# Mixture of experts behind windowed attention: weights in pairs of blocks, a fifth round turned by VectorE

## The chip, the cores and the metric

The kernel runs on one core of a Trainium2 chip. The metric is device time in microseconds (us), the median over the runs shown. A profile is one more execution, recorded by the hardware profiler: TensorE (PE), VectorE (DVE), ScalarE (ACT), GpSimd (POOL), SyncE (SP, which here only issues DMAs) and the DMA queues.

## The reference

Attention over 8 batches of 8 heads (576 positions, 64 columns a head), four heads with a window of 32 positions and four with 32 positions at a stride of 4. Its output, 4608 rows of 512 columns, is the input of a layer with 8 experts, in which each row goes to one expert and each expert takes exactly 576 rows:

```python
    logits = x @ w_gate
    flat = logits.flatten()
    order = np.argsort(-flat)
    for idx in order:
        tok, e = (int(idx) // E, int(idx) % E)
        if assigned[tok] >= 0 or counts[e] >= cap:
            continue
        assigned[tok] = e
        counts[e] += 1
    for e in range(E):
        mask = assigned == e
        h = np.maximum(x[mask] @ w1[e], 0.0)
        out[mask] = h @ w2[e]
```

An expert's w1 is 512 x 1024 and its w2 1024 x 512, both float32, 2 MB each.

## The kernel before, in words

**Attention** (`attention`) fills the first 175 us, writes its rows x to DRAM (`xd`) and keeps the gate's logits. Nothing in it is changed.

**Rounds.** In each of eight rounds the router finds the expert that fills next and the list of its 576 rows. A round's search is eight steps, one after the other: nine small matmuls on PE (`counts`, L835) and a DVE chain of about 2 us (`step`, from L880). Then the expert's number goes to SP's registers (`fetch`), and the list is built (`settle`, `listing`: DVE compares, 18 small matmuls at L1174 into `ptx`, then `idx` at L1200). Later rounds' searches run while earlier experts are computed.

**Rows.** POOL gathers the listed rows in five blocks (four of 128 rows, one of 64) by indirect DMAs. For the matmuls they must stand with the 512 columns on the partitions. In the first five rounds (`gather`) PE transposes them: four matmuls a block at L1391 into PSUM. From round QUARTERS = 5 on (counted from 0: the sixth) `spread` does it without PE: gathered rows go to a buffer (two alternate), from there to a DRAM scratch (L1415), come back in four quarters of the columns (L1419), and DVE turns them in blocks of 32 x 32 (L1425). The columns then stand in another order on the partitions, so w1 is read from a second copy in that order, `w1q`. In both ways ACT rounds the block to `xh` and DVE computes the rest, `xl` (L1237, L1238). There is one `xh` and one `xl`, so these splits wait until the expert before has read its rows for the last time.

**Weights** (`weights`). A block is 128 x 512 values, 256 KB; w1 and w2 have eight blocks each. SP loads it into a `raw` buffer (L1255; eight for w1, four for w2), ACT rounds it to the high part, DVE subtracts to get the low part. In the first expert's w2 and the second's w1 and w2 (`ADDED`) DVE is spared: ACT writes the negated high part (L1264) and a DMA issued by POOL adds `raw` to it (L1266). Each part has eight buffers, one expert's worth. In the first two rounds a POOL memset of one element of a `raw` buffer (L1246), queued behind the gathers, holds the loads from block 3 or 4 on (`AHEAD_W`), since the load of that buffer, and all that SP has queued behind it, waits for it.

**Products** (`expert`). First product: for each of eight blocks f of the hidden layer and two column ranges j (256 and 320 rows of x), twelve matmuls into `ph` (L1455): high by high, low by high, high by low, over four parts of the 512 columns. ACT takes relu and rounds (`hb`), DVE the rest (L1476). Second product: for each of the five blocks of rows, over the eight f, three matmuls (L1500; two for the block of 64 rows, L1503 and L1505) into `py`, from where ACT copies and POOL scatters to the output.

**The order** is made when the kernel is built: each operation is listed with its engine, a cost, what it depends on and a boost; `Schedule.run` gives every engine its next operation by due time, and lets one that would be due later go first where it fits into idle time (up to a tolerance, 100 ns on DVE). The engines then execute their queues in order and wait by semaphores for the data alone. Costs given there decide the order and nothing else. B_W is the boost of weights, B_C that of a search, lower from round QUARTERS on.

Of the kernel before, what the change touches and what calls it, by code (L numbers as in the profile page):

```python
# [8 lines left out]
F32 = mybir.dt.float32  # L9
F32R = mybir.dt.float32r  # L10
# [4 lines left out]
AF = mybir.ActivationFunctionType  # L15
OP = mybir.AluOpType
# [6 lines left out]
DM = H * D  # L23
NE, FF = 8, 1024
# [14 lines left out]
TOL_DVE, TOL_ACT, TOL_POOL, TOL_PE, T_W = 100, -50, 200, 500, 730  # L39
T_P, T_S, AHEAD = 310, 2200, 5  # L40
B_L, B_G, B_T, B_X, B_H, B_HL, B_Y, B_S, B_W = 23000, 27000, 15000, 0, 20000, 17000, 28000, -15000, 1500
RAW1, D_R, NQ, AHEAD_W = 8, 262, (2, 2), (3, 4)
KB, QUARTERS, POOLED, T_B, T_H, B_R = 8, 5, range(0), 5000, 2500, 20000
ADDED, T_A, T_G, T_L = (("2", 0), ("1", 1), ("2", 1)), 4500, 4500, 3500
NS, B_E, DIRECT = (2, 2), 3000, 7
B_C = (0, 2500, *(20000 + -16000 * (r >= QUARTERS) for r in range(2, 8)))
# [1158 lines left out]
def moe(tc, ctx, C, R, xd, ROWS, w1, w1q, w2, out):  # L1205
    nc = tc.nc
# [4 lines left out]
    NF, ND = FF // 128, DM // 128  # L1211
# [6 lines left out]
    def ring(pool, shape, dtype, name, n):  # L1218
        return Ring([pool.tile(shape, dtype, name=f"{name}{i}") for i in range(n)])
# [1 line left out]
    PHR = [ring(ps, [128, 512], F32, f"ph{j}", 2) for j in range(2)]  # L1221
    PYR = ring(ps, [128, DM], F32, "py", 2)
    PTR = ring(ps, [128, 512], F32, "ptx", 1)
    RAW = {n: ring(pw, [128, 512], F32, "raw" + n, k) for n, k in (("1", RAW1), ("2", 4))}
    WH, WL = ({n: ring(pw, [128, 512], F32R, "w" + n + x, NF) for n in ("1", "2")} for x in "hl")
    XG = [pw.tile([128, DM // (1 + (i == 4))], F32, name=f"xg{i}") for i in range(NM + 2)]
    XU = [[] for _ in XG]
    XH, XL = (pw.tile([128, ND, CAP], F32R, name=n) for n in ("xh", "xl"))
# [9 lines left out]
    sub = lambda e, o, a, b: e.tensor_tensor(o, a, b, op=OP.subtract)  # L1238
    E, gemm1_end, x_users, got, gate = {}, {}, {}, {}, {}

    def weights(n, r, f, deps):

        raw, old, use = RAW[n].take()
        if n == "1" and r < len(AHEAD_W) and f == AHEAD_W[r]:

            gate[r] = op("POOL", 100, lambda: nc.gpsimd.memset(raw[:1, :1], 0.0), [got[r, 1], *old], B_G)  # L1246
        if r in gate:
            deps = [*deps, gate[r]]

        def load():  # L1250
            if n == "1":
                src = (w1 if r < QUARTERS else w1q)[bass.ds(E[r], 1), f].rearrange("o p d f -> p (o d f)")
            else:
                src = w2[bass.ds(E[r], 1), f * 128:f * 128 + 128, :].rearrange("o p d -> p (o d)")
            nc.sync.dma_start(raw, src)  # L1255

        ld = op("SP", 60, load, [*deps, *old], dma=T_W, lat=T_L if n == "1" and r == 1 and r in gate else 0)
        h, oldh, useh = WH[n].take()
        l, oldl, usel = WL[n].take()
        first = n == "1" and r == 0  # L1260
        hi = op("ACT", 525, lambda: act(h, raw), [ld, *oldh, st["rows"] if first else None], B_W)
        if (n, r) in ADDED:
            use.append(hi)
            ne = op("ACT", 525, lambda: nc.scalar.activation(l, h.bitcast(F32), AF.Copy, scale=-1.0), [hi, *oldl], B_W)  # L1264
            useh.append(ne)
            lo = op("POOL", 1040, lambda: nc.gpsimd.dma_start(l, raw, accum_op=OP.add), [ne], B_W, lat=T_A)  # L1266
            use.append(lo)
        elif n == "2" and r >= 2 and f in POOLED:
            lo = op("POOL", 1350, lambda: sub(nc.gpsimd, l, raw, h), [ld, hi, *oldl], B_W)
            use += [hi, lo]  # L1270
        else:
            lo = op("DVE", 600, lambda: sub(nc.vector, l, raw, h), [ld, hi, *oldl, st["list"] if first else None], B_W)
            use += [hi, lo]
        useh.append(lo)
        return h, l, hi, lo, useh, usel


    def chain(eng, cost, fn, deps, boost=None):
        return op(eng, cost, fn, deps, B_C[len(scan)] if boost is None else boost)
# [262 lines left out]
    def round_(r):  # L1542
        e = None
        if r:
            e = search(r) if r < NE - 1 else chain("DVE", 980, R.last, [st["fetch"], st["need"]])
        en = st["fetch"] = EN[r] = op("SP", 100, lambda: fetch(r, R.eidx), [e])
        ix, BOX[r] = settle(r, e)
        X[r] = gather(r, ix, BOX[r])
        if r < NE - 2:
            lv, gf = st["next"]  # L1550
            oc = (chain("ACT", 1055, lambda: R.copies(R.oh, nc.scalar), [lv]) if r else
                  chain("DVE", 640, lambda: R.copies(R.oh, nc.vector), [lv]))
            st["next"] = [oc, gf]
        W[r] = [weights("1", r, f, [en]) for f in range(NF)]

    round_(0)
    for r in range(NE):
        W2 = [weights("2", r, f, [EN[r], X[r][-1][0] if r == 1 else None]) for f in range(NF)]
        expert(r, X[r], BOX[r], W[r], W2)
        if r + 1 < NE:  # L1560
            round_(r + 1)
# [8 lines left out]
def layout(inputs):  # L1570
# [3 lines left out]
    seq = lambda x: x[:, 4:].reshape(B, 4, SR, DIL, D).transpose(0, 1, 3, 2, 4).reshape(B, 4, S, D)  # L1574
    rowwise = lambda x: ones(x.transpose(0, 2, 1, 3)).reshape(B, NB, 64, 4 * (D + 1)).transpose(0, 2, 1, 3).reshape(B, 64, -1)
    ones = lambda x: np.concatenate([x, np.ones(x.shape[:-1] + (1,), x.dtype)], -1)
    cb, _, cf, _ = consts()
    d = {
        "in_qp": plain(q[:, :4]), "in_kp": plain(k[:, :4]), "in_vp": rowwise(v[:, :4]),
        "in_qd": plain(seq(q)), "in_kd": plain(seq(k)), "in_vd": rowwise(seq(v)),  # L1580
        "in_moe_w_gate": np.asarray(inputs["moe_w_gate"]),
        "in_moe_w1": w1.reshape(NE, DM // 128, 128, FF // 128, 128).transpose(0, 3, 2, 1, 4),
        "in_moe_w1q": w1.reshape(NE, 4, DM // 128, 32, FF // 128, 128).transpose(0, 4, 1, 3, 2, 5).reshape(NE, FF // 128, 128, DM // 128, 128),
        "in_moe_w2": w2,
        "in_cb": cb, "in_cf": cf,
    }
# [54 lines left out]
```

## Time and profile before

| what | us |
| --- | --- |
| median of three runs | 658.03 |
| the runs | 656.75, 658.03, 662.26 |
| the profiled execution | 661.16 |
| its span, first to last instruction | 659.4 |

The profiled execution is one run with the profiler on; its durations belong to its own 661.16 us. A row that groups instructions gives line, engine, operation, tile written and tiles read, the count, then busy time, mean duration, and idle time before them. Matmuls overlap in PE's pipeline, so a matmul's duration is longer than the distance from its start to the next one's.

### The profile page before, as it was taken

What the parts mean: (1) busy time and instruction counts of PE and PEld (TensorE: products, weight loads), DVE (VectorE), ACT (ScalarE), POOL (GpSimd) and SP (SyncE); (2) the same over time, 40 slices, a digit from 0 to 9 for tenths busy, and PEclk for the clock granted to TensorE, in tenths of its full rate; (3) what the DMA queues carried; (4) which work ended last, traced back from release to release, by engine and by line L of the source; (5) the groups of instructions that cost most, each with busy time, mean ns of one, the idle gap of its engine ahead of it and who ended that gap; (6) DMA issues with size and microseconds to landing.
All of it is one profiled execution on the core that took longest, in us unless ns stands there. A gap on an engine that the chain in (4) does not pass through costs nothing.

```text
span 659.4 us, 18449 instructions
## 1 busy us (share of the span) xinstructions
PE 622.0 (94%) x7140; PEld 543.8 (82%) x7142; DVE 463.4 (70%) x1560; ACT 307.1 (47%) x675; POOL 208.4 (32%) x316
## 2 busy tenths in 40 slices
PE   6899899999748999999999999999999999999996
PEld 4788788888545988898799789879978988988985
DVE  4677577876676784689799888989898864724210
ACT  5667567566203824765336245325415624524311
POOL 6447555745003316434103113012212133011011
PEclk8999899999957999999999999999999999999999
DMA  8988699885106737997127135217714977403001
GB/s 237 261 234 239 205 280 260 257 214 178 45 33 215 150 68 205 250 193 267 67 71 247 61 93 194 85 52 252 216 57 161 281 243 229 127 32 105 1 25 48
DMA packets 61448, 106.11 MB, mean 161 GB/s; under 512 B 8368, under 2 KB 25264, under 8 KB 61360
## 3 DMA queue, kind: packets, MB, share of 16 engines
q1 hardware_dynamic: 52016, 79.75, 40.2%
q0 software_dynamic: 9344, 25.17, 14.3%
q8 instruction: 56, 0.92, 0.6%
q14 instruction: 32, 0.26, 0.2%
HBM read 76.19 MB, written 22.41 MB: 150 GB/s over the span
## 4 chain that ended last, share of the span: by engine, by line
PE 84%; DVE 5%; issue 5%; DMA 2%; ACT 2%; POOL 1%; SPq 0%; POOLq 0%; DVEq 0%; ACTq 0%
PE ph L1455 32%; PE py L1500 24%; PE px L543 5%; PE pS L531 4%; PE px L602 3%; PE py L1503 2%; PE py L1505 2%; PE pz L835 2%; PE ptx L1391 1%; PE pS L526 1%; PE pm L519 1%; PE pm L515 1%; PE pz L919 1%; PE px L628 1%; PE pm L468 1%
## 5 line engine op out<-in xcount | busy, mean ns | idle before, releaser
L1500 PE MATMUL py<-w2h,hb 128*128 128x512 f32 x512 | 168.6, 397 | 0.0
L1455 PE MATMUL ph<-xh,w1h 128*128 128x256 f32 (+1 forms) x512 | 138.7, 302 | 0.0
L1455 PE MATMUL ph<-xh,w1l 128*128 128x256 f32 (+1 forms) x512 | 136.8, 298 | 0.0
L1455 PE MATMUL ph<-xl,w1h 128*128 128x256 f32 (+1 forms) x512 | 136.4, 297 | 0.0
L1500 PEld LDWEIGHTS py<-w2h,hb 128*128 128x128 f32 x512 | 96.1, 188 | 19.0
L1237 ACT ACTIVATE hb<-ph 128x256 fp32r<-128x256 f32 (+2 forms) x192 | 59.8, 346 | 86.9 <-PE ph L1455 85.9
L1500 PE MATMUL py<-w2l,hb 128*128 128x512 f32 x256 | 99.8, 390 | 0.0
L1526 POOL DMA_INDIRECT out<-y,idx x40 | 39.7, 994 | 186.0 <-ACT y L1237 141.3
L1455 PEld LDWEIGHTS ph<-xh,w1h 128*128 128x128 f32 x512 | 92.0, 191 | 0.5
L1455 PEld LDWEIGHTS ph<-xh,w1l 128*128 128x128 f32 x512 | 92.1, 191 | 0.0
L1455 PEld LDWEIGHTS ph<-xl,w1h 128*128 128x128 f32 x512 | 92.1, 191 | 0.0
L1476 DVE SCALAR_TENSOR_TENSOR hb<-ph,hb 128x320 fp32r<-128x320 f32 (+1 forms) x128 | 57.0, 454 | 30.5 <-ACT hb L1237 29.4
L1237 ACT ACTIVATE y<-py 128x512 f32<-128x512 f32 (+1 forms) x40 | 23.9, 597 | 108.5 <-PE py L1500 95.1
L485 ACT ACTIVATE E<-pS 128x384 f32<-128x384 f32 x96 | 44.7, 491 | 28.0 <-PE pS L531 27.3
L1500 PEld LDWEIGHTS py<-w2l,hb 128*128 128x128 f32 x256 | 48.2, 188 | 8.6
L543 PE MATMUL px<-v,E 128*64 128x65 f32 x1152 | 48.7, 224 | 5.2 <-issue 3.8
L531 PE MATMUL pS<-q,k 128*64 128x64 f32 x1152 | 52.6, 227 | 0.5 <-issue 0.5
L543 PEld LDWEIGHTS px<-v,E 128*64 128x64 f32 x1152 | 42.4, 137 | 9.8 <-issue 5.8
L311 POOL COPY v<-v 32x520 f32<-32x520 f32 (+2 forms) x56 | 34.2, 633 | 46.6 <-DMA v<-in_vp 17.1
L531 PEld LDWEIGHTS pS<-q,k 128*64 128x64 f32 x1152 | 48.0, 142 | 0.7 <-issue 0.7
L1238 DVE TENSOR_TENSOR w2l<-raw,w2h 128x512 fp32r<-128x512 f32 x48 | 31.8, 685 | 18.8 <-ACT w2h L1237 17.8
L1237 ACT ACTIVATE w1h<-raw 128x512 fp32r<-128x512 f32 x64 | 38.6, 627 | 3.4 <-DMA raw<-in_moe_w 3.4
(218 smaller groups left out, 1121.4 us busy)
## 6 DMA issues: line engine op xcount, KB each, us to landing
raw<-in_moe_w SPq DMA_DIRECT2D x104, 256.0 KB, 4.4
raw<-in_moe_w1q SPq DMA_DIRECT2D x24, 256.0 KB, 4.3
qs<-in_qp SPq DMA_DIRECT2D x16, 288.0 KB, 3.8
k<-in_kp SPq DMA_DIRECT2D x16, 288.0 KB, 4.5
qs<-in_qd SPq DMA_DIRECT2D x16, 288.0 KB, 5.7
k<-in_kd SPq DMA_DIRECT2D x16, 288.0 KB, 5.1
xd<-xs SPq DMA_DIRECT2D x8, 512.0 KB, 5.7
w2l<-raw POOLq DMA_DIRECT2D x16, 256.0 KB, 4.3
```

The lines of the kernel that those rows point to most:

```text
L311: f(t[:32, c0 + 1:c1 + 1], t[96:, c0:c1])
L485: e = self.op("ACT", 475, lambda j=j, pS=pS: nc.scalar.activation(self.E[:, 3 * j:3 * j + 3].rearrange("p c x -> p (c x)"), pS.tile[:, :38 ...
L531: x = nc.tensor.matmul(pS[64 * h:64 * h + 64, k, :, h], self.K[:, 32 * g:32 * g + 64], self.Q[:, g], start=False, stop=True, skip_group_ch ...
L543: x = nc.tensor.matmul(px[64 * h:64 * h + 64, c - c0, a], self.E[:, k, 64 * a:64 * a + 64], self.V[:, k, 2 * self.ui + a], start=True, sto ...
L602: x = nc.tensor.transpose(pt.tile[:, 128 * (c - c0):128 * (c - c0) + 128], xs[:, c, 2 * ui:2 * ui + 2].rearrange("p a d -> p (a d)"), C["i ...
L835: nc.tensor.matmul(o, self.ohr[:, j].rearrange("p r x -> p (r x)"), self.G[:, 4 * j:4 * j + 4, :w], start=(j == 0), stop=(j == NCH // 4 - 1))
L1237: act = lambda o, i, f=AF.Copy: nc.scalar.activation(o, i, f)
L1238: sub = lambda e, o, a, b: e.tensor_tensor(o, a, b, op=OP.subtract)
L1455: nc.tensor.matmul(o, a[:, d * 128:d * 128 + 128], b[:, d, c0:c1], start=((d, i) == pairs[0]), stop=((d, i) == pairs[-1]))
L1476: hl = op("DVE", 335 if j == 0 else 400, lambda: nc.vector.scalar_tensor_tensor(hb[:, CAP + c0:CAP + c1], o, 0.0, hb[:, c0:c1], op0=OP.max ...
L1500: nc.tensor.matmul(py, x, w, start=(f + i == 0), stop=(f == NF - 1 and i == 2))
L1526: s = nc.gpsimd.indirect_dma_start(out=out, out_offset=bass.IndirectOffsetOnAxis(ap=box[0][:n, m:m + 1], axis=0), in_=y[:n], in_offset=None)
```

## The change

A weight tile becomes 128 x 1024, two blocks: one DMA of 512 KB, one ACT operation for the high part, one DVE operation (or ACT and adding DMA) for the low part, and products use halves of it. `raw` buffers keep their bytes (four for w1, two for w2), as do the parts (four tiles each). w1 lies in DRAM in pairs, so that a partition's 1024 values are contiguous; w2 is read as two rows of 512. `AHEAD_W` becomes (2, 2): the memset holds the third pair. QUARTERS becomes 4: the fifth round's rows go through the DRAM scratch and are turned by DVE, that expert reads `w1q`, and that round's search gets the lower boost. The costs given to the scheduler change with the sizes. A way to split on POOL that no tile used is gone.

```diff
-RAW1, D_R, NQ, AHEAD_W = 8, 262, (2, 2), (3, 4)
-KB, QUARTERS, POOLED, T_B, T_H, B_R = 8, 5, range(0), 5000, 2500, 20000
+RAW1, D_R, NQ, AHEAD_W = 8, 262, (2, 2), (2, 2)
+KB, QUARTERS, T_B, T_H, B_R = 8, 4, 5000, 2500, 20000
...
-    RAW = {n: ring(pw, [128, 512], F32, "raw" + n, k) for n, k in (("1", RAW1), ("2", 4))}
-    WH, WL = ({n: ring(pw, [128, 512], F32R, "w" + n + x, NF) for n in ("1", "2")} for x in "hl")
+    RAW = {n: ring(pw, [128, 1024], F32, "raw" + n, k) for n, k in (("1", RAW1 // 2), ("2", 2))}
+    WH, WL = ({n: ring(pw, [128, 1024], F32R, "w" + n + x, NF // 2) for n in ("1", "2")} for x in "hl")
...
-    def weights(n, r, f, deps):
+    def weights(n, r, g, deps):
 
         raw, old, use = RAW[n].take()
-        if n == "1" and r < len(AHEAD_W) and f == AHEAD_W[r]:
+        if n == "1" and r < len(AHEAD_W) and g == AHEAD_W[r]:
...
-                src = (w1 if r < QUARTERS else w1q)[bass.ds(E[r], 1), f].rearrange("o p d f -> p (o d f)")
+                src = (w1 if r < QUARTERS else w1q)[bass.ds(E[r], 1), g].rearrange("o p x -> p (o x)")
+                nc.sync.dma_start(raw, src)
             else:
-                src = w2[bass.ds(E[r], 1), f * 128:f * 128 + 128, :].rearrange("o p d -> p (o d)")
-            nc.sync.dma_start(raw, src)
-
-        ld = op("SP", 60, load, [*deps, *old], dma=T_W, lat=T_L if n == "1" and r == 1 and r in gate else 0)
+                src = w2[bass.ds(E[r], 1), g * 256:g * 256 + 256, :].rearrange("o (u p) d -> p (o u) d", p=128)
+                nc.sync.dma_start(raw.rearrange("p (u d) -> p u d", u=2), src)
+
+        ld = op("SP", 60, load, [*deps, *old], dma=2 * T_W, lat=T_L if n == "1" and r == 1 and r in gate else 0)
...
-        hi = op("ACT", 525, lambda: act(h, raw), [ld, *oldh, st["rows"] if first else None], B_W)
+        hi = op("ACT", 950, lambda: act(h, raw), [ld, *oldh, st["rows"] if first else None], B_W)
...
-            lo = op("DVE", 600, lambda: sub(nc.vector, l, raw, h), [ld, hi, *oldl, st["list"] if first else None], B_W)
+            lo = op("DVE", 1140, lambda: sub(nc.vector, l, raw, h), [ld, hi, *oldl, st["list"] if first else None], B_W)
...
-        return h, l, hi, lo, useh, usel
-
+        return [(h[:, x:x + 512], l[:, x:x + 512], hi, lo, useh, usel) for x in (0, 512)]
...
-        W[r] = [weights("1", r, f, [en]) for f in range(NF)]
+        W[r] = [x for g in range(NF // 2) for x in weights("1", r, g, [en])]
```

Three places show how the order moves. In the names below, `raw10` to `raw17` are w1's raw buffers and `raw20` to `raw23` w2's.

SP's queue at the first expert, before: the three first blocks of w1, then the load that waits for POOL's memset, and everything else behind it.

```order
L1255 DMA raw11_3702<-in_moe_w1 128x512
L1255 DMA raw12_3703<-in_moe_w1 128x512
L1255 DMA raw13_3704<-in_moe_w1 128x512 [waits Pool_49]
L1255 DMA raw14_3705<-in_moe_w1 128x512
L1255 DMA raw20_3709<-in_moe_w2 128x512
L1255 DMA raw21_3710<-in_moe_w2 128x512
```

The same place now; the row ahead of these loads `raw10`.

```order
L1253 DMA raw11_3702<-in_moe_w1 128x1024
L1256 DMA raw20_3705<-in_moe_w2 128x2x512
L1256 DMA raw21_3706<-in_moe_w2 128x2x512
L1253 DMA raw12_3703<-in_moe_w1 128x1024 [waits Pool_49]
L1253 DMA raw13_3704<-in_moe_w1 128x1024
```

Two pairs of w2 have moved ahead of the load that waits.

PE's queue in the fourth expert's second product, before (`w2h`, `w2l` are the parts of w2, `hb` the hidden layer, `xg` gathered rows):

```order
L1500 MATMUL py_3699<-w2h_3726,hb_3756 128x512
L1500 MATMUL py_3699<-w2l_3742,hb_3756 128x512
L1391 MATMUL ptx_3700<-const_63,xg_3745 128x128 x4
L1500 MATMUL py_3699<-w2h_3727,hb_3757 128x512
L1500 MATMUL py_3699<-w2l_3743,hb_3757 128x512
```

The same products now:

```order
L1497 MATMUL py_3699<-w2h_3713,hb_3734 128x512
L1497 MATMUL py_3699<-w2l_3721,hb_3734 128x512
L1497 MATMUL py_3699<-w2h_3714,hb_3735 128x512
L1497 MATMUL py_3699<-w2l_3722,hb_3735 128x512
```

The transposition is gone, and so are the four others of that round; the searches between these products stay.

DVE's queue at the end of the third expert's first product, before, from the list of the fourth round (`idx`) on; rows of the search and the list are left out. `hb4` and `hb5` are the last two hidden blocks.

```order
L1476 SCALAR_TENSOR_TENSOR hb4_3758<-ph00_3694,hb4_3758 128x256
L1238 TENSOR_TENSOR w2l3_3740<-raw23_3712,w2h3_3724 128x512
L1200 SCALAR_TENSOR_TENSOR idx_6291<-t1_6292 64x5 x2
L1238 TENSOR_TENSOR w2l4_3741<-raw20_3709,w2h4_3725 128x512
L1238 TENSOR_TENSOR w2l5_3742<-raw21_3710,w2h5_3726 128x512
L1238 TENSOR_TENSOR w2l6_3743<-raw22_3711,w2h6_3727 128x512
L1238 TENSOR_TENSOR w2l7_3744<-raw23_3712,w2h7_3728 128x512
```

The same place now:

```order
L1473 SCALAR_TENSOR_TENSOR hb4_3736<-ph00_3694,hb4_3736 128x256
L1200 SCALAR_TENSOR_TENSOR idx_6195<-t1_6196 64x5 x2
L1238 TENSOR_TENSOR w2l0_3719<-raw20_3705,w2h0_3711 128x1024
L1238 TENSOR_TENSOR w2l1_3720<-raw21_3706,w2h1_3712 128x1024
L1473 SCALAR_TENSOR_TENSOR hb5_3737<-ph01_3695,hb5_3737 128x256
L880 STREAM_TRANSPOSE Q_6249<-pz_92 128x128
L1238 TENSOR_TENSOR w2l2_3721<-raw20_3705,w2h2_3713 128x1024
L1238 TENSOR_TENSOR w2l3_3722<-raw21_3706,w2h3_3714 128x1024
```

Before, the splits of blocks 0 to 2 had gone long ago; now the first pair of the eight blocks stands behind the list, and the third pair, which uses the first one's raw buffer, behind a step of the next search.

## Rows read from the trace of the kernel before

**Rows 1.** The page: the span, and section 1, busy us and share.

```profile
span 659.4 us, 18449 instructions
...
PE 622.0 (94%) x7140; PEld 543.8 (82%) x7142; DVE 463.4 (70%) x1560; ACT 307.1 (47%) x675; POOL 208.4 (32%) x316
```

**Rows 2.** Windows by stage: stretch, length, busy us per engine, PE's clock, DMA share, GB/s.

```profile
208.70:268.00 59.30, 59.28 (x420) 52.63 (x416) 40.81 (x151) 30.92 (x65) 20.94 (x27) 0.97 0.68 170
...
386.50:444.20 57.70, 57.70 (x424) 50.43 (x421) 50.57 (x184) 23.39 (x52) 11.33 (x15) 1.00 0.35 115
...
552.00:603.10 51.10, 51.10 (x306) 46.22 (x305) 24.16 (x44) 21.15 (x50) 7.41 (x14) 1.00 0.36 109
```

**Rows 3.** Windows: the first 3.5 us of products (same columns).

```profile
208.77:212.28 3.51, 3.51 (x22) 3.39 (x18) 3.13 (x11) 1.12 (x2) 0.00 (x0) 0.51 0.98 312
```

**Rows 4.** PE's waits, 190 to 660 us: us in total, times, longest.

```profile
PE ptx L1180 <- POOL rx L1160: 3.5, 1, 3.5
PE ptx L1391 <- DMA xg<-xd,idx: 2.0, 1, 2.0
PE py L994 <- DVE pra L992: 0.8, 1, 0.8
```

**Rows 5.** Timeline of PE at a transposition: start, us, instruction.

```profile
417.94 0.60 PE L1391 MATMUL ptx<-const,xg 128*128 128x128 f32 x4
418.29 0.48 PE L1500 MATMUL py<-w2h,hb 128*128 128x512 f32 x1
418.61 0.39 PE L1500 MATMUL py<-w2l,hb 128*128 128x512 f32 x1
418.84 0.62 PE L1500 MATMUL py<-w2h,hb 128*128 128x512 f32 x2
```

**Rows 6.** Groups of instructions by form: busy us, mean ns, idle before.

```profile
L1237 ACT ACTIVATE w1h<-raw 128x512 fp32r<-128x512 f32 x64 | 38.6, 627 | 3.4 <-DMA raw<-in_moe_w 3.4
...
L1238 DVE TENSOR_TENSOR w1l<-raw,w1h 128x512 fp32r<-128x512 f32 x56 | 37.0, 687 | 0.1
...
L1425 DVE STREAM_TRANSPOSE xg<-xg 128x512 f32<-128x512 f32 x12 | 8.3, 701 | 0.7 <-DMA xg<-rows 0.7
...
L972 ACT ACTIVATE ohr<-oh 128x1152 bf16<-128x1152 bf16 x5 | 5.8, 1161 | 1.9 <-DVE oh L951 1.9
...
L1093 DVE TENSOR_TENSOR Lt<-Lt,cap 128x288 f32<-128x288 f32 x6 | 2.8, 459 | 0.2
```

**Rows 7.** Windows of 1 us at the start of the experts (columns as in rows 2).

```profile
196.00:197.00 1.00, 0.26 (x6) 0.36 (x7) 1.00 (x2) 0.78 (x2) 0.81 (x2) 0.50 0.75 238
197.00:198.00 1.00, 1.00 (x21) 0.99 (x20) 0.87 (x2) 0.20 (x1) 0.52 (x1) 0.50 0.96 342
...
202.00:203.00 1.00, 1.00 (x5) 0.29 (x3) 0.93 (x5) 0.00 (x0) 0.69 (x2) 0.98 0.66 209
```

**Rows 8.** Timeline of POOL, 199 to 207 us: the first of five gathers, and the memset.

```profile
199.72 1.45 POOL L1377 DMA_INDIRECT xg<-xd,idx  x1 [2.20 <-DVE idx L1192]
...
206.62 0.09 POOL L1246 MEMSET raw<- 1x1 f32 x1
```

**Rows 9.** Timeline of PE, 203 to 209.5 us: third transposition, first products.

```profile
208.03 0.63 PE L1391 MATMUL ptx<-const,xg 128*128 128x128 f32 x4 [1.99 <-DMA xg<-xd,idx]
...
208.77 1.12 PE L1455 MATMUL ph<-xh,w1h 128*128 128x256 f32 x4
```

**Rows 10.** Tile w2l on DVE, 320 to 362 us: ns min/median/max, first and last start.

```profile
L1238 DVE TENSOR_TENSOR w2l<-raw,w2h x8: 677/681/684, 327.2 to 358.3; 128x512 fp32r<-128x512 f32 x8
```

**Rows 11.** Timeline of DVE: the end of the fourth round's list.

```profile
352.46 0.33 DVE L1200 SCALAR_TENSOR_TENSOR idx<-t 64x5 int32<-64x5 f32 x2
```

**Rows 12.** Tile raw on SP, 297 to 300 us, then 206 to 212 us.

```profile
DMA to landing us min/median/max: 2.6/3.3/4.3
...
DMA to landing us min/median/max: 3.3/4.6/5.0
```

**Rows 13.** Timeline of PE: the third expert's second product begins.

```profile
355.39 0.39 PE L1500 MATMUL py<-w2h,hb 128*128 128x512 f32 x1
```

**Rows 14.** Tile w2l on POOL, 274 to 294 us: the adding DMAs.

```profile
DMA to landing us min/median/max: 3.3/4.5/5.1
```

More of the change, by code (lines that the diff above doesn't have):

```diff
@@ L1260, in weights @@
         first = n == "1" and r == 0
-        hi = op("ACT", 525, lambda: act(h, raw), [ld, *oldh, st["rows"] if first else None], B_W)
+        hi = op("ACT", 950, lambda: act(h, raw), [ld, *oldh, st["rows"] if first else None], B_W)
         if (n, r) in ADDED:
             use.append(hi)
-            ne = op("ACT", 525, lambda: nc.scalar.activation(l, h.bitcast(F32), AF.Copy, scale=-1.0), [hi, *oldl], B_W)
+            ne = op("ACT", 950, lambda: nc.scalar.activation(l, h.bitcast(F32), AF.Copy, scale=-1.0), [hi, *oldl], B_W)
             useh.append(ne)
-            lo = op("POOL", 1040, lambda: nc.gpsimd.dma_start(l, raw, accum_op=OP.add), [ne], B_W, lat=T_A)
+            lo = op("POOL", 1040, lambda: nc.gpsimd.dma_start(l, raw, accum_op=OP.add), [ne], B_W, lat=T_A + T_W)
             use.append(lo)
-        elif n == "2" and r >= 2 and f in POOLED:
-            lo = op("POOL", 1350, lambda: sub(nc.gpsimd, l, raw, h), [ld, hi, *oldl], B_W)
-            use += [hi, lo]
         else:
-            lo = op("DVE", 600, lambda: sub(nc.vector, l, raw, h), [ld, hi, *oldl, st["list"] if first else None], B_W)
+            lo = op("DVE", 1140, lambda: sub(nc.vector, l, raw, h), [ld, hi, *oldl, st["list"] if first else None], B_W)
             use += [hi, lo]
         useh.append(lo)
-        return h, l, hi, lo, useh, usel
+        return [(h[:, x:x + 512], l[:, x:x + 512], hi, lo, useh, usel) for x in (0, 512)]
     def chain(eng, cost, fn, deps, boost=None):
@@ L1553, in round_ @@
             st["next"] = [oc, gf]
-        W[r] = [weights("1", r, f, [en]) for f in range(NF)]
+        W[r] = [x for g in range(NF // 2) for x in weights("1", r, g, [en])]
     round_(0)
     for r in range(NE):
-        W2 = [weights("2", r, f, [EN[r], X[r][-1][0] if r == 1 else None]) for f in range(NF)]
+        W2 = [x for g in range(NF // 2) for x in weights("2", r, g, [EN[r], X[r][-1][0] if r == 1 else None])]
         expert(r, X[r], BOX[r], W[r], W2)
@@ L1576, in layout @@
     ones = lambda x: np.concatenate([x, np.ones(x.shape[:-1] + (1,), x.dtype)], -1)
+    pairs = lambda x: x.reshape(NE, FF // 256, 2, 128, DM).transpose(0, 1, 3, 2, 4).reshape(NE, FF // 256, 128, 2 * DM)
     cb, _, cf, _ = consts()
@@ L1581, in layout @@
         "in_moe_w_gate": np.asarray(inputs["moe_w_gate"]),
-        "in_moe_w1": w1.reshape(NE, DM // 128, 128, FF // 128, 128).transpose(0, 3, 2, 1, 4),
-        "in_moe_w1q": w1.reshape(NE, 4, DM // 128, 32, FF // 128, 128).transpose(0, 4, 1, 3, 2, 5).reshape(NE, FF // 128, 128, DM // 128, 128),
+        "in_moe_w1": pairs(w1.reshape(NE, DM // 128, 128, FF // 128, 128).transpose(0, 3, 2, 1, 4)),
+        "in_moe_w1q": pairs(w1.reshape(NE, 4, DM // 128, 32, FF // 128, 128).transpose(0, 4, 1, 3, 2, 5)),
         "in_moe_w2": w2,
```

## The prediction

> **What bounds the kernel now.** I read the page's busy times first, then the windows by stage, the waits of TensorE (PE), a few microseconds of its timeline, and last the start of the experts' part with VectorE (DVE), GpSimd (POOL) and the DMA. The page shows PE busy for 94% of a span of 659.4 us [rows 1]. The windows say where it is not: attention before 175 us and the routing up to 208.7 us. From there on it is busy from edge to edge, 59.28 of 59.30 us for the first expert and 51.10 of 51.10 for the seventh [rows 2], and the granted clock is full (2.4 GHz) except in the first 3.5 us, where it stood at 1.2 GHz [rows 3]. The view of PE's waits from 190 us on lists 3.5 us in the routing, 2.0 us for a gather at the start of the first expert [rows 4], others of at most 0.8, and after 209.7 us the view has not one row. So the experts' 445 us are PE's own work, and DVE, at 70% over the span, delays nobody there. Two things can move the time: instructions that PE no longer executes, and waits that do not exist today.
>
> The seventh expert, with nothing but products, takes 51.1 us, the fourth 57.7 [rows 2]. The rest is searches, list building and transpositions, all standing between products. One transposition (four matmuls on 128 rows) is seen at 417.94: the next product starts 0.35 us later, and that product takes 0.32 instead of 0.23, so the block costs 0.44, of which 0.09 is charged to any interruption [rows 5].
>
> **The change part by part.**
>
> *Fifth round turned by DVE.* Its five transposition blocks, 417.9 to 430 us, leave PE. That is 5 x 0.35 = 1.75 us, and 5 x 0.09 = 0.45 more if the interruptions went too. They don't: counting in the orders the places where something stands between products after the first one, I find 75 before and 75 after. Searches that shared a place with a transposition now stand alone, and the first search has moved behind the first products. Term: -1.75. What it adds lies elsewhere: five DVE transposes of at most 0.70 us each [rows 6], five writes and twenty reads on SP's queue, and for the gathers the two row buffers. All of it must end before the fifth expert starts (442 us here). The new list of that round is built 40 matmuls into the fourth expert, some 45 us ahead; the sixth round takes the same path today, and PE doesn't wait for it. Taken at 0; without that cover a late transpose would cost its own delay. The smaller boost of that round's search moves it within the same slack: 0.
>
> *Two blocks at a time.* A DVE split of 512 columns takes 0.687, an operation on 288 columns 0.459 [rows 6], that is 1.02 ns a column, so 1024 columns take about 1.21: between one (0.69) and two (1.37). The 56 of w1 become 28, 38.5 us of DVE become 33.9; w2's follow in proportion. ScalarE (ACT) goes from 0.627 for 512 to about 1.05, by the 1.161 of a 1152-column operation [rows 6]. SP issues half as many weight DMAs. None of that is on PE's path: the saving is worth 0, covered by the products. What is worth something is the grain, in three places.
>
> *Start of the first expert.* SP's new order puts two loads of w2, 1 MB, ahead of the load that waits for POOL's memset; only that later one has the wait, so they run at once. Today 768 KB move before the gathers; after, 2.1 MB. Loads reached 342 GB/s, and 238 in the microsecond in which they began, so from about 196.3 [rows 7]; 2.1 MB last 6.1 us, to about 202.4. The first gather is issued at 199.72 and its instruction takes 1.45 [rows 8], so for about 1.3 us both want the DMA engines. A gather alone moved 209 GB/s [rows 7]; together they want 551 and get 342, and 1.3 x (1 - 342/551) = 0.5 us are lost. Bounds: 0, if gathers are held by something else, and 1.3, if they stand behind all loads. The gathers are on the path: PE's third transposition waited for its rows until 208.03, products from 208.77 [rows 9]. I take +0.5. The search that stood between moves behind the products at equal cost.
> The Trainium skill (DMA: Bandwidth & Descriptors, section Queues, rings and completion order) has each DMA engine take turns between queues, packet by packet. By that rule the gathers give up about half of the 1.3 us, 0.65, and the sum below would be 0.15 higher. No run here shows yet whether loads and gathers share like that.
>
> *Third expert, w2.* With 0.6 us splits DVE filled gaps between search steps: the eight w2 splits of that round begin at 327.2 and end at 359.0 [rows 10]. The new order has all four pairs behind the fourth round's list, since 1.2 us fits no gap. There are only two raw buffers, so the third pair's load can't begin before the first pair's split ends. By hand: the list ends at 352.2 (today 352.8 with a split of 0.7 ahead of it [rows 11]); first split to 353.4; load of 512 KB 3.4 (2.6 for 256 KB alone [rows 12], and 0.7 for as much again at 342 GB/s) to 356.9; ACT to 358.0, DVE to 359.2. PE starts these products at 355.39 [rows 13] and needs the third pair after twelve of them (2.7), one search (0.3) and one transposition (0.44), its low part at 359.1. With a semaphore's delay on each step it is 0.3 late, and the fourth pair, whose ACT and DVE work queues behind, 0.5. Term: +0.8. Bounds: 0, and 2.3 if loads take the 5.0 us seen under traffic [rows 12], which delays the chain by 1.5. Queued behind the split on DVE are the search and the hidden activations of the last block, needed only 5 us later.
>
> *Second expert, w2.* Its low parts come from accumulating DMAs, landing 3.3 to 5.1 us after issue [rows 14]; two stages of twice the size end, by the same counting, 1.6 to 3 us before their use. 0, bounds 0 and 1.5. For searches that find DVE or ACT in a longer instruction (0.5 us more each) I take +0.2, bounds 0 and 0.6.
>
> Sum: -1.75 + 0.5 + 0.8 + 0.2 = -0.25 us. Against the profiled execution's 661.16 us (span 659.4 and 1.8 around it) that gives 660.9. That execution was 3.1 us above the median of the three runs, so on the median 658.03 it gives 657.8.
>
> **The rivals.**
>
> A. The start costs more and the change loses. Place: the third gather before the first products. If gathers stand behind all loads (+1.3) and PE's longer idle stretch brings a second stretch at half clock, as in 208.77 to 212.28 (3.5 us at 0.51 [rows 3], so 1.7 lost), the start costs 3.0: -1.75 + 3.0 + 1.0 = +2.25, 660.3. It decides as soon as the third transposition starts more than 0.75 us later than 208.03. For it: nothing guards the two loads. Against: the last two gathers already overlap the loads that follow the memset at 206.62 [rows 8], and PE does not wait for them.
>
> B. The coarse grain costs more. With all upper bounds in the second and third expert, -1.75 + 0.5 + 2.3 + 1.5 + 0.6 = +3.15, 661.2. For it: two raw buffers instead of four make load, ACT and DVE a chain. Against: PE waited nowhere today under orders made by the same rules.
>
> C. No wait appears, and the start is free: -1.75, 656.3; with fewer interruptions too, -2.2, 655.8. For it: today's empty list of waits.
>
> D. The fifth round's rows come late. Not the transposes but the way through DRAM would then set the start of the fifth expert: gather, write, read, with five blocks going through two row buffers. By the landing times [rows 12], at most 5.0 us a transfer, three turns of gather and write through the first buffer and a read come to at most 35 us of the 45. Each microsecond beyond the 45 is lost in full; 10 us late would give about 668. Against: the sixth round already goes this way [rows 4].
>
> The change can also fail to do what it says: fewer, larger loads shorten nothing where loads are hidden, and that is in the sum already.
>
> **How the numbers follow.** The forecast's own case, net -1.5 to +1, has 0.45 (656.5 to 659.0); A 0.2, B 0.15, C 0.15, D 0.05. The range takes in C at its low end (655.8) and B at its high end (661.2), with the spread of the runs shown (656.75 to 662.26) on top: 654.0 to 662.5. A difference of 1% (6.6 us) is about what a measurement of this kernel can tell from no change. No case reaches 651.5 by rows, so faster gets 0.04; slower needs D, or A and B together with something unseen, 0.11; the same 0.85.
>
> **What would show it.** In the profile after: no transpositions on PE between products of the fourth expert, and its window shorter by about 2 us; loads and gathers sharing the DMA between 201 and 202.5 us, the third transposition near 208.5; in the third expert a PE wait of under 1 us for w2's third and fourth pair, and no wait in the fifth. I am wrong if PE waits are listed by whole microseconds, if the first products start after 209.6, or if the experts' part shrinks by more than 2.2 us.

## The result, and the profile after

The changed kernel takes 666.83 us (median of 20 runs, 660.5 to 674.5), the kernel before 662.43 (20 runs, 656.53 to 665.0). Three of the changed kernel's runs, from 672.42 us up, were slow ones, and the ratio leaves them out. It is 1.0069, with a 95% interval of 1.0043 to 1.0095. The prediction's 658.03 us was the median of three runs, 4.4 below that of the twenty; on it the ratio gives 662.6 us (660.9 to 664.3). The forecast was no change, 657.8, within 654.0 to 662.5. The change makes the kernel slower by 0.4 to 1.0%, and the forecast's range ends inside 660.9 to 664.3.

The profiled execution took 669.36 us, 2.5 above the median of its kernel, and the one before 1.3 below, so the stages add up to more than the difference of the medians (8.4 us in the first six experts against 4.4). The page, as in [rows 1]:

```profile
span 667.5 us, 18049 instructions
...
PE 624.7 (94%) x7122; PEld 543.1 (81%) x7122; DVE 464.0 (70%) x1513; ACT 297.0 (45%) x599; POOL 204.9 (31%) x304
```

PE is busy for 94% in both; the page hides the loss. Windows from the first product of one expert to that of the next show it (columns as in [rows 2]). Before, the first six experts but for the fifth, which takes 54.94 us before and 55.03 after:

```profile
208.77:267.98 59.21, 59.19 (x417) 52.54 (x414) 40.81 (x151) 30.85 (x65) 20.94 (x27) 0.97 0.67 170
267.98:327.86 59.88, 59.86 (x469) 52.27 (x467) 51.91 (x197) 35.97 (x75) 21.45 (x29) 1.00 0.72 192
327.86:386.57 58.71, 58.71 (x450) 51.35 (x446) 52.72 (x191) 23.44 (x53) 11.22 (x16) 1.00 0.35 113
386.57:444.24 57.67, 57.67 (x422) 50.36 (x419) 50.57 (x185) 23.32 (x52) 11.33 (x15) 1.00 0.35 115
...
499.18:551.97 52.79, 52.77 (x346) 47.18 (x344) 37.77 (x104) 22.92 (x52) 16.59 (x20) 1.00 0.75 235
```

After, the same five, and then two short stretches that are read below:

```profile
208.66:266.42 57.76, 57.76 (x423) 51.31 (x422) 40.73 (x150) 28.01 (x50) 15.95 (x21) 1.00 0.57 148
266.42:332.22 65.80, 62.27 (x477) 54.10 (x476) 52.90 (x204) 32.93 (x56) 17.59 (x23) 0.97 0.65 181
332.22:395.62 63.40, 60.72 (x436) 51.80 (x434) 54.23 (x192) 22.70 (x44) 11.87 (x15) 0.97 0.31 105
395.62:450.85 55.23, 55.21 (x397) 48.55 (x396) 48.29 (x154) 22.40 (x44) 11.72 (x16) 1.00 0.51 163
...
505.88:560.22 54.34, 53.62 (x346) 47.55 (x344) 37.17 (x100) 21.75 (x44) 18.99 (x21) 1.00 0.72 228
...
274.00:275.00 1.00, 1.00 (x5) 1.00 (x5) 0.86 (x7) 0.97 (x2) 0.54 (x1) 0.50 0.00 0
...
370.00:371.00 1.00, 1.00 (x4) 0.79 (x3) 0.96 (x4) 0.26 (x1) 0.00 (x0) 0.50 1.03 387
```

The fourth expert, where the transpositions left PE, gained 2.4 us (57.67 to 55.23), and the first 1.5, since its first products ran at full clock this time. The second lost 5.9, the third 4.7, the sixth 1.6; one search, about 0.3 us of PE, has moved from the third to the second. PE's five longest waits from 212 us on, where before the view has no row (`G` from DVE and `ohr` from ACT are what a search's matmuls read, `rx` and `ob` what a list's read; `spacer` is a one-element memset on POOL ahead of each scatter):

```profile
PE ph L1452 <- ACT xh L1237: 1.9, 1, 1.9
PE pz L835 <- ACT ohr L972: 1.6, 1, 1.6
PE py L1497 <- DVE w2l L1238: 1.5, 2, 0.8
PE py L1497 <- ACT w2h L1237: 0.8, 1, 0.8
PE ptx L1174 <- POOL spacer L1522: 0.6, 1, 0.6
```

**The second expert's wait for xh.** ACT's timeline shows the cause one step back (its last four rows are read further down):

```profile
270.11 0.59 ACT L1237 ACTIVATE y<-py 64x512 f32<-64x512 f32 x1 [2.81 <-DMA out<-y,idx]
...
271.95 0.38 ACT L1237 ACTIVATE xh<-ptx 128x256 fp32r<-128x256 f32 x1
...
308.70 1.06 ACT L1237 ACTIVATE w1h<-raw 128x1024 fp32r<-128x1024 f32 x1 [1.91 <-DMA raw<-in_moe_w]
...
310.95 1.15 ACT L972 ACTIVATE ohr<-oh 128x1152 bf16<-128x1152 bf16 x1
...
362.56 1.06 ACT L1237 ACTIVATE w2h<-raw 128x1024 fp32r<-128x1024 f32 x1 [2.15 <-DMA raw<-in_moe_w]
366.03 1.06 ACT L1237 ACTIVATE w2h<-raw 128x1024 fp32r<-128x1024 f32 x1 [2.40 <-DMA raw<-in_moe_w]
```

ACT's copy of the first expert's last output block stood 2.8 us for a scatter to land: there are three `y` buffers, and the fifth block takes the second one's. In ACT's queue the rounding `xh` stands behind that copy and a pair of w1, and PE waits for it. On POOL the second block's scatter now comes late:

```profile
259.48 1.02 POOL L1267 DMA_DIRECT2D w1l<-raw  x1
...
260.81 1.06 POOL L1523 DMA_INDIRECT out<-y,idx  x1 [0.27 <-issue]
...
356.85 1.34 POOL L1374 DMA_INDIRECT xg<-xd,idx  x1 [3.58 <-PE ph L1452]
...
362.57 0.90 POOL L1374 DMA_INDIRECT xg<-xd,idx  x1 [0.30 <-issue]
```

It is issued at 260.8, behind five gathers, the memset and an adding DMA of 512 KB; before, it stood ahead of the gathers (issued at 252.6). PE stood idle for 1.9 us, to 272.4, and after that its granted clock was 0.50 (the row of 274 to 275), the lower level, 1.2 GHz.

**The second expert's wait for ohr** (1.6 us, to 312.15) comes from ACT's queue too. `ohr` begins there at 310.95, behind two pairs of the third expert's w1, the first of which waited 1.9 us for its load. Before, ACT had rounded the blocks of that w1 by 306.8 and began `ohr` at 306.89.

**The third expert's w2.** DVE's timeline, from the end of the fourth round's list:

```profile
355.74 0.33 DVE L1200 SCALAR_TENSOR_TENSOR idx<-t 64x5 int32<-64x5 f32 x2
356.11 1.23 DVE L1238 TENSOR_TENSOR w2l<-raw,w2h 128x1024 fp32r<-128x1024 f32 x1
...
357.65 1.22 DVE L1238 TENSOR_TENSOR w2l<-raw,w2h 128x1024 fp32r<-128x1024 f32 x1
...
363.65 1.22 DVE L1238 TENSOR_TENSOR w2l<-raw,w2h 128x1024 fp32r<-128x1024 f32 x1 [1.67 <-issue]
367.12 1.23 DVE L1238 TENSOR_TENSOR w2l<-raw,w2h 128x1024 fp32r<-128x1024 f32 x1 [2.24 <-ACT w2h L1237]
```

All four splits stand behind the list. The first frees its buffer at 357.3, the third pair reaches ACT at 362.6; the second frees its own at 358.9, the fourth reaches ACT at 366.0: 5.2 and 7.2 us from split to ACT, in the time in which the five gathers are issued. PE's three waits for it (2.3 us; the first and the last are shown) and, behind them, a second stretch at 1.2 GHz:

```profile
364.93 0.50 PE L1497 MATMUL py<-w2l,hb 128*128 128x512 f32 x1 [0.76 <-DVE w2l L1238]
...
368.40 0.55 PE L1497 MATMUL py<-w2l,hb 128*128 128x512 f32 x1 [0.76 <-DVE w2l L1238]
368.74 1.05 PE L1497 MATMUL py<-w2h,hb 128*128 128x512 f32 x2
```

### The profile page after: what moved, and what is told of

The parts are those of the page before. It is cut to its first block, busy times and chain, and to the rows that moved or that the text cites. A ratio compares the mean times of both kernels' runs of the same rounds, so it can differ in the third digit from the quotient of the medians.

```text
span 667.5 us, 18049 instructions
## 1 busy us (share of the span) xinstructions
PE 624.7 (94%) x7122; PEld 543.1 (81%) x7122; DVE 464.0 (70%) x1513; ACT 297.0 (45%) x599; POOL 204.9 (31%) x304
## 4 chain that ended last, share of the span: by engine, by line
PE 69%; DVE 11%; DMA 8%; issue 6%; ACT 4%; POOL 1%; SPq 1%; POOLq 0%; DVEq 0%; ACTq 0%
PE ph L1452 22%; PE py L1497 20%; PE px L543 4%; PE pS L531 4%; DMA raw<-in_moe_w 3%; PE px L602 3%; PE py L1500 2%; PE py L1502 2%; PE pz L835 2%; PE pS L526 1%; PE pm L519 1%; DVE hb L1473 1%; PE pm L515 1%; DMA xg<-rows 1%; DVE w2l L1238 1%
## 5 line engine op out<-in xcount | busy, mean ns | idle before, releaser
L1523 POOL DMA_INDIRECT out<-y,idx x40 | 41.2, 1030 | 170.7 <-ACT y L1237 135.3
L1406 POOL DMA_INDIRECT xg<-xd,idx x20 | 24.9, 1246 | 74.4 <-DMA rows<-xg 60.5
L1238 DVE TENSOR_TENSOR w2l<-raw,w2h 128x1024 fp32r<-128x1024 f32 x24 | 29.1, 1216 | 22.0 <-ACT w2h L1237 20.3
```

The source lines that it names most:

```text
L1406: nc.gpsimd.indirect_dma_start(out=rows[:n], out_offset=None, in_=xd, in_offset=bass.IndirectOffsetOnAxis(ap=box[0][:n, m:m + 1], axis=0))
L1523: s = nc.gpsimd.indirect_dma_start(out=out, out_offset=bass.IndirectOffsetOnAxis(ap=box[0][:n, m:m + 1], axis=0), in_=y[:n], in_offset=None)
```

## The experiments

**The two halves of the change.** The letters in this part are those of the texts written ahead of the runs, and not those of the prediction's rivals. Theory A is the prediction's: turning gains, coarse weights cost. Rival B: the rows' detour through DRAM costs.

Turning alone, on the kernel before:

```diff
-KB, QUARTERS, POOLED, T_B, T_H, B_R = 8, 5, range(0), 5000, 2500, 20000
+KB, QUARTERS, POOLED, T_B, T_H, B_R = 8, 4, range(0), 5000, 2500, 20000
```

> The kernel before with one edit: QUARTERS 5 to 4, so the fifth round's rows go through the DRAM scratch; weights stay in single blocks. Theory A (the coarse weights cost, the turning gains): five transposition blocks leave PE and no wait comes, 1.8 to 2.7 us less than before, ratio 0.996 to 0.997, and the fourth expert's window about 2.5 us shorter. Rival B (the detour of the rows through DRAM costs: its loads, writes and transposes make other work late): ratio 1.000 or more, with a PE wait for xh or xl near the start of the fifth expert or a later search.

Ratio 1.0060 (1.0035 to 1.0085): against A. PE's three longest waits in experts two to six:

```profile
PE pz L835 <- DVE G L849: 2.0, 2, 1.4
PE ptx L1174 <- ACT rx L1164: 0.9, 1, 0.9
PE py L1500 <- ACT w2h L1237: 0.9, 1, 0.9
```

`rx`, `w2h` and 0.6 us of the waits for `G` stand in the third expert: searches, lists and weights come late there. No row names the fifth expert's xh or xl, where B looked for them. The longer wait for `G`, 1.4 us at 475.4, does stand in a search of the fifth expert, just behind a row block that DVE turned, and that is as B has it. So B is not excluded, but it doesn't explain the third expert: something else is at work there.

Pairs alone, the changed kernel with QUARTERS back at 5:

> The changed kernel with one edit: QUARTERS back to 5, so only the weights in pairs remain. Theory A: all waits of the changed kernel in the second and third expert stay, and the five transpositions come back: 6 to 8 us above before, ratio 1.009 to 1.012. Rival B: the pairs cost nothing or little, ratio at most 1.004.

Ratio 1.0051 (1.0022 to 1.0079), between the two. The wait for xh is there (1.6 us), the waits for w2 are not. The two halves alone cost 0.6 and 0.5%, together 0.7; the intervals don't exclude that they add up. The waits don't: `ohr` is in neither half's list. The tile `w2l` on DVE, 325 to 400 us, tells why w2 is in time here:

```profile
L1238 DVE TENSOR_TENSOR w2l<-raw,w2h x4: 1215/1221/1227, 329.2 to 361.2; 128x1024 fp32r<-128x1024 f32 x4
```

The first pair is split at 329.2, in a gap between search steps. Counted from the third expert's first product (329.90 here, 332.22 in the changed kernel) that is some 25 us earlier than in the changed kernel. So 1.2 us does fit a gap.

Pairs for w1 alone, and for w2 alone (the other in single blocks, with the buffers and `AHEAD_W` that belong to it), fifth round turned:

> The changed kernel with w2 back in single blocks (four raw buffers, eight parts), w1 in pairs. Theory A1 (the third expert's w2 chain is the larger cost: load, ACT and DVE through two raw buffers): its PE waits for w2 and the half-clock stretch behind them go, 4 to 5 us below the changed kernel, ratio to before 0.998 to 1.002; the second expert's wait for xh and the search's wait for ohr stay. Rival A2 (most of it is w1's pairs): less than 2 us below the changed kernel, ratio 1.004 or more.

> The changed kernel with w1 back in single blocks (eight raw buffers, memset gates as before), w2 in pairs. Theory A1: the third expert's waits for w2 stay (3 us of waits, 1 us of half clock), the second expert's wait for xh and the search's wait for ohr go: ratio to before 1.000 to 1.005. Rival A2: with w1's pairs gone nearly all of the loss goes, ratio 0.996 to 0.999.

Ratios 1.0093 (1.0058 to 1.0128) and 1.0215 (1.0174 to 1.0256). The first can't be told from the changed kernel, which is A2's case; the second is well above it, which neither A1 nor A2 allows. In the first PE waits 2.0 us for xh, in the second 4.2 for xl, 2.4 for G, 2.1 for ohr. Each mixture is another order by the planner; such runs don't divide the loss between w1 and w2.

**Where the searches stand.** Theory P: the planner gives an operation its due time from all that hangs on it. Rows that go through DRAM hang far more time on the fifth round's list, so that list, the searches ahead of it and those of the round before are due sooner. In the orders, turning alone moves the eight searches of the fourth round forward by 14 to 36 products and the fifth's list from 123 products into the fourth expert to 36. In the changed kernel these searches stand within three products of the same places. To move the searches without turning, on the kernel before:

```diff
-B_C = (0, 2500, *(20000 + -16000 * (r >= QUARTERS) for r in range(2, 8)))
+B_C = (0, 2500, 20000, 24000, 24000, 4000, 4000, 4000)
```

> The kernel before with one edit: the boost of the fourth and fifth rounds' searches goes from 20000 to 24000. Nothing is turned by VectorE that wasn't, no weight changes; the 16 searches of these rounds stand on PE where the turned kernel has the first eight of them (45, 57, 69, 84, 98, 108 products into the second product of the second expert, 16 and 36 into the first of the third) and some of the rest. Theory P (what costs is that these searches and lists are pulled forward, into stretches where DVE and ACT have no slack): 2 to 4 us slower, ratio 1.003 to 1.006, with PE waits for G, rx or w2 in the third expert. Rival B (the way of the rows through DRAM costs by itself): no change, ratio 0.998 to 1.002.

Ratio 1.0074 (1.0042 to 1.0107): P, and more than it asked. With nothing turned and no pair, PE waits in the third expert, whose window grows from 58.71 us to 60.75:

```profile
PE pz L835 <- DVE G L849: 1.0, 1, 1.0
PE py L1500 <- DVE w2l L1238: 0.8, 1, 0.8
...
324.94:385.69 60.75, 58.88 (x436) 51.04 (x434) 53.87 (x197) 23.34 (x52) 11.56 (x16) 1.00 0.34 109
```

This execution (660.02 us) is among the fastest of its kernel (659.97 to 669.13), so it shows a part of the loss. And the edit does more than turning does: the fourth round's list now stands 126 products into the third expert, against 162 before and in the changed kernel. It shows that early searches cost, not how much they cost in the changed kernel.

The reverse, turning with the searches left in place, on the kernel before with QUARTERS = 4:

```diff
+B_C = (0, 2500, 20000, 20000, 16000, 4000, 4000, 4000)
-        g = op("POOL", 1250, get, [ix, *XU[NM + m % 2]], B_G, lat=T_B)
+        g = op("POOL", 1250, get, [ix, *XU[NM + m % 2]], B_G, lat=T_B - 2000 * (r == 4))
-        sd = op("SP", ..., B_R, dma=T_W, lat=T_H)
+        sd = op("SP", ..., B_R, dma=T_W * (r > 4), lat=T_H - 1000 * (r == 4))
```

> The kernel before with the fifth round turned by VectorE, but its searches left where they are: the planner's assumed waits for that round's rows are cut (2 us less for a gather, 3 us less for a write and a read) and its search boost is 16000, so that all searches and lists up to the fourth round's stand on PE as before, and the fifth round's list 90 instead of 123 products into the fourth expert (36 with the plain edit). Theory P: the waits in the third expert are gone and five transpositions with them, 1.5 to 2.5 us faster than before, ratio 0.996 to 0.998, unless rows come late at the fifth expert (then a PE wait for xh there, of 2 to 6 us). Rival B: the loss of the plain edit stays, ratio 1.004 or more.

Ratio 1.0028 (0.9999 to 1.0057). The third expert's waits are gone, but the kernel is not faster: a wait of 1.3 us for G and 0.5 us for w2l now stand in the fourth. Ahead of that G, DVE stood 1.7 us for ACT's `w2h`, whose load came 3.0 us late; DVE turned no rows just there. Why the load is late wasn't tried. P is right on the third expert and was too hopeful on the gain; the ratio can be told neither from 1 nor from that of turning alone. The same two edits on the changed kernel:

> The changed kernel with the same two planner edits (assumed waits cut, search boost 16000): searches and lists up to the fourth round's stand on PE as with the pairs alone. Theory P: the third expert's waits for w2 (3.1 us) and the half-clock stretch behind them go, the second expert's wait for xh stays; 2 to 5 us below the changed kernel, ratio to before 1.000 to 1.004. Rival A (the grain of w2 alone makes the chain late): the third expert's waits for w2 stay, ratio 1.006 or more.

Ratio 1.0010 (0.9984 to 1.0037), as P says, and below the changed kernel's interval: `w2l` is split from 330.2 on, no wait for w2 or `ohr` is listed, the wait for xh stays at 1.6 us:

```profile
L1238 DVE TENSOR_TENSOR w2l<-raw,w2h x5: 1217/1219/1225, 330.2 to 389.4; 128x1024 fp32r<-128x1024 f32 x5
```

**The scatter.** Pairs alone with one boost:

```diff
-            puts[r, m] = op("POOL", 1200, put, [c], B_S, lat=2300)
+            puts[r, m] = op("POOL", 1200, put, [c], 60000 if (r, m) == (0, 1) else B_S, lat=2300)
```

> Pairs alone (fifth round not turned) with one edit: the first expert's second output block has a boost that puts its scatter on POOL ahead of the first adding DMA and the gathers of the second round, where the kernel before had it ahead of the gathers. Theory S (with pairs that scatter slipped behind five gathers, an adding DMA and a memset, landed 15 us later, and held ACT's copy of the last output block, and behind it xh and PE): the PE wait of 1.6 us for xh at the start of the second expert is gone, 1.5 to 3.5 us below pairs alone, ratio to before 0.999 to 1.003. Rival (ACT is late there by the length of its pair operations): a wait of 1 us or more for xh stays, ratio as pairs alone, 1.005.

Ratio 1.0002 (0.9973 to 1.0032), and no wait for xh: theory S. The boost moves the scatter and its memset alone; DVE, ACT and SP execute the same sequence in both traces. Its counterpart, the kernel before with that scatter and its memset put behind the gathers and the memset by hand:

> The kernel before with one instruction pair moved: the scatter of the first expert's second output block (and the one-element memset ahead of it) stands on POOL behind the second round's five gathers and the memset instead of ahead of them; every other engine's order is the same, weights in single blocks. Theory S: its landing moves from 256 to about 267 to 270 us, ACT's copy of the last output block waits 1 to 3 us for it, and xh and PE behind it: 1 to 3 us slower, ratio 1.0015 to 1.005, with a PE wait for xh at the start of the second expert. Rival (with single blocks ACT has the slack, since only pairs are long): no wait, ratio 0.999 to 1.001.

Ratio 1.0006 (0.9975 to 1.0038), no wait for xh: S as stated falls, the rival holds. What differs is the adding DMA, which in the pairs also stands ahead. Two more, in which POOL's queue alone differs from its base: single blocks with the scatter behind two adding DMAs, and pairs with it behind the gathers but ahead of the adding DMA.

> The kernel before (single blocks) with the scatter of the first expert's second output block moved on POOL behind the second round's gathers, the memset and two adding DMAs of 256 KB; nothing else moved. Theory S2 (a scatter behind an adding DMA lands late, whatever the size of the blocks): a PE wait for xh of 1 to 3 us at the start of the second expert, ratio 1.002 to 1.006. Rival S3 (what holds it in the pairs is the four loads of 512 KB that SP starts within 2 us): no wait, ratio 0.998 to 1.002.

> Pairs alone with the same scatter between the memset and the adding DMA of 512 KB that stood ahead of it, so still behind the gathers; nothing else moved. Theory S2: no wait for xh, ratio 0.999 to 1.002. Rival S3: the wait of 1 to 2 us stays, ratio 1.003 to 1.006.

Ratios 1.0031 (0.9998 to 1.0064) and 0.9996 (0.9965 to 1.0028): S2, for the pairs. In `scatter_behind` PE waits 1.0 us for xh, as S2 says, but its ratio can't be told from 1, and its other waits (1.7 us for a gather at the start, 1.6 for xl late in the second expert) are not the scatter's. ACT's copy in single blocks, scatter issued at 262.79:

```profile
270.55 0.59 ACT L1237 ACTIVATE y<-py 64x512 f32<-64x512 f32 x1 [2.34 <-DMA out<-y,idx]
```

and in pairs, scatter issued at 260.20:

```profile
267.96 0.60 ACT L1237 ACTIVATE y<-py 64x512 f32<-64x512 f32 x1 [0.22 <-DMA out<-y,idx]
```

Counted from the second round's first gather, the scatter is issued after 6.8 us in the two kernels without this wait or nearly so (`scatter_late`, `pairs_mid`), after 7.9 in pairs alone and 8.7 in `scatter_behind`. Where ACT waits for it, the wait ends 7.8 to 9.0 us after issue; in `scatter_late` ACT's copy begins 7.4 us after it without a wait. One or two microseconds of POOL's queue decide, in either size of block; the adding DMA takes them. In `pairs_mid` the view of waits from 212 to 560 us is empty, as before the change.

**Together.** The changed kernel with the scatter's boost alone, then with both edits (twice):

> The changed kernel with the scatter's boost alone (early searches left in): PE's order is word for word the changed kernel's. Theories S and P: the second expert's wait for xh goes, the waits of the third expert for w2 and the search's wait for ohr stay: 2 to 4 us below the changed kernel, ratio to before 1.002 to 1.005.

> Both edits together on the changed kernel: assumed waits cut and boost 16000 for the fifth round, and the scatter's boost. Theories S and P: neither wait is left, five transpositions are gone: below the pairs with the scatter's boost by 0.5 to 2 us, 1 to 3 us below before, ratio 0.995 to 0.999. Rival: turning by VectorE is worth nothing even so (its work on DVE makes searches in the fourth expert wait for G): ratio 1.000 to 1.002.

> The same kernel as with both planner edits, once more: if it is faster than before, the ratio is again between 0.993 and 0.999.

Ratios 1.0037 (0.9999 to 1.0074), 0.9961 (0.9930 to 0.9992) and 1.0002 (0.9974 to 1.0030). The first keeps its waits for w2l (1.3 us) and ohr (0.7), as expected, and has 1.4 us at the sixth expert's last list. With both edits the waits for xh, w2 and `ohr` are all gone. The first profiled execution has 1.0 us for G in the fourth expert, the sign that the rival named, and the second, of the same kernel, has not: a wait of that size comes and goes from one execution to the next. The kernel with both edits is faster than the changed one; that it beats the kernel before is not shown, since the second measurement doesn't repeat the first. Its fourth and sixth expert, in the second:

```profile
387.09:442.64 55.55, 55.42 (x406) 48.80 (x405) 50.24 (x171) 22.45 (x44) 13.90 (x16) 1.00 0.50 160
497.65:551.81 54.16, 53.81 (x346) 47.62 (x344) 36.61 (x94) 21.74 (x44) 17.21 (x20) 1.00 0.73 229
```

and those of `pairs_mid`, where the fifth round is not turned:

```profile
385.28:442.75 57.47, 57.47 (x422) 50.47 (x419) 49.52 (x174) 22.38 (x44) 13.19 (x15) 1.00 0.34 115
497.87:550.63 52.76, 52.74 (x346) 47.25 (x344) 36.73 (x98) 21.51 (x44) 16.98 (x20) 1.00 0.73 235
```

The fourth expert gains 1.9 us and the sixth gives back 1.4. In these two executions turning is worth half a microsecond, which the ratios can't tell from nothing. The longer sixth goes with the turning: it takes 53.6 to 56.2 us in the eight kernels here that turn the fifth round, 52.8 to 53.3 in the seven that don't. Why wasn't tried; in the changed kernel PE waits there 0.6 us at the last list.

## Why the prediction was wrong

*The transpositions.* Right in place, and near in size: -1.75 predicted, -2.4 in the fourth expert's window. The sixth grew by 1.6 meanwhile, which had no term.

*Their cover.* This step failed. "Taken at 0" stood on the list being ready 45 us ahead, and "moves it within the same slack: 0" on the search's boost. The prediction gave the list's new place, 40 products into the fourth expert, and priced only what comes after it. The searches ahead of it and those of the fourth round move too, in the second and third expert, where PE reaches them before DVE and ACT are done. Moving such searches, and one list further than the change does, cost 0.74% by itself (4.9 us on 658.03), more than the transpositions are worth. With the searches put back, the changed kernel's loss went from 0.69% to 0.10%. A step moved early was counted as free; its cover was sought at its end instead of where it now stands.

*Third expert, w2.* The chain through two raw buffers was seen and had its term, +0.8; the window lost 4.7. The cause given, "since 1.2 us fits no gap", is refuted by the pairs alone, whose first pair is split at 329.2. The earlier searches took the gap: put back, they leave the first split at 330.2. The size failed in the load: 3.4 us assumed, 5.0 at most, 5.2 and 7.2 seen, beside the gathers of the fourth round, which [rows 12] don't contain. And no term of the sum had the clock: 2.3 us of waits in small pieces brought 3 us at 1.2 GHz, in which a product takes 0.43 instead of 0.23.

*Second expert.* Taken at 0 by the adding DMAs' landing before their use. No wait names them. Of the 5.9 us lost, 1.6 are the wait for `ohr`, which went with the searches put back. For most of the rest, what was late is an instruction that the change doesn't touch, behind them on POOL. The step looked at the queue of the data and not at what else stands in the issuing engine's queue; the prediction's own rule, to name what is queued behind, was applied to DVE and not to POOL. Putting that scatter back took the pairs alone from 1.0051 to 1.0002.

*The start.* +0.5 predicted; the third transposition began at 208.30, inside the 0.75 us that rival A needed and near the forecast's 208.5:

```profile
204.85 1.12 PE L1388 MATMUL py<-const,xg 128*128 128x128 f32 x4 [2.14 <-DMA xg<-xd,idx]
...
208.30 0.60 PE L1388 MATMUL ptx<-const,xg 128*128 128x128 f32 x4
208.66 0.60 PE L1452 MATMUL ph<-xh,w1h 128*128 128x256 f32 x3
```

From the first gather's issue to the first product it took 9.25 us (199.41 to 208.66) against 9.05 before (199.72 to 208.77 [rows 8, 9]). The number fits, but by another path, and that is luck: PE waited for rows at the first transposition and no longer at the third. The stretch at 1.2 GHz followed that wait (granted 0.50 from 205 to 208; the first transposition takes 1.12 us, the third 0.60) and was over before the first product. That is the first expert's gain of 1.5 us, which had no term.

The sharing of the DMA can be read too. The first gather's instruction ran from 199.41 to 201.39. The rows are, in this order: the kernel before from its first gather's issue on, 199.72 to 201.85, with no load in flight; the changed kernel from 200 to 202; the changed kernel from 202 to 203 (`q0` are POOL's DMAs, `q1` SP's):

```profile
DMA packets 0, 0.00 MB, mean 0 GB/s; under 512 B 0, under 2 KB 0, under 8 KB 0
...
q1 hardware_dynamic: 374, 0.73, 98.3%
...
q0 software_dynamic: 46, 0.18, 62.6%
q1 hardware_dynamic: 67, 0.11, 29.6%
```

Even with no load in flight that gather moved no packet for 2.1 us; the first came 0.7 us after its instruction's end (201.17 to 201.89). The prediction counted 1.3 us of common demand from that end on, so about half of it was not there. From 202 on both queues move packets. The Trainium skill (DMA: Bandwidth & Descriptors, section Queues, rings and completion order) has each DMA engine take turns between the queues that have work for it. The rows of 202 to 203 agree, with 46 packets of gathers beside 67 of loads. Beside the loads the gather's instruction took 1.98 us instead of 1.45, and its block reached PE 5.4 us after issue instead of 3.9.

*The rivals.* B (+3.15, 661.2, chance 0.15) came nearest. Its chain of load, ACT and DVE in the third expert is there; its waits for adding DMAs are not, and no rival had the searches or the scatter, so the nearness is partly luck. Its "PE waited nowhere today under orders made by the same rules" was the reason to put it low. An empty list of waits says nothing of how much slack there is: 4000 more of boost, in `search_early`, and it isn't empty any more.

## What to carry to other kernels

Where a planner sets the order, a longer chain behind an operation pulls everything ahead of it forward: compare the orders upstream of the edit, not only at it, and price the stretch into which things move. In an in-order queue, ask of every instruction near a changed one what it now stands behind and whose buffer it frees. Undoing one half of such a change is no clean experiment; moving one instruction by hand, with all other queues word for word the same, is.

## What was not expected of the hardware

A scatter of 256 KB that took 3.3 us to land before the change (252.64 to 255.91) took 7.8 to 9.3 us when issued 8 us later, among gathers, adding DMAs and loads; in the kernel before, too, the two issued at 263.3 and 265.1 took 7.0 and 7.9. With no other DMA in flight a gather's first packet came 2.2 us after its issue (199.72 to 201.89). And the granted clock fell to 1.2 GHz after PE had been idle for 1.9 us in one piece, and also after 2.3 us in three pieces of 0.8 with products between them.
